# Pooled attention feeding a SoLU feed-forward block: SyncE's plain transfers moved to slots of their own, and one matmul group put first in every second slot

## The chip, the core and the metric

The kernel runs on one core of one Trainium2 chip. The metric is the device time of one launch in microseconds (us), the median of several runs. TensorE (PE) multiplies matrices, VectorE (DVE), ScalarE (ACT) and GpSimd (POOL) work element by element, SyncE (SP) only issues DMAs. All engines run their own instruction lists and wait for each other by semaphores.

## What is computed

```python
# q: (4, 12288, 128), kv: (4, 384, 32, 128), w_sr: (128, 128)
kv_pool = kv.reshape(B, H // 4, 4, W // 4, 4, C).mean(axis=(2, 4))
k = v = kv_pool.reshape(B, -1, C) @ w_sr               # 768 keys a batch
a = softmax(q @ k.T / sqrt(C))
x = (a @ v).reshape(B * S, 128)                        # 49152 tokens
h = x @ w_in                                           # 128 -> 1024
solu = h * softmax(h)
ln = (solu - mean(solu)) / sqrt(var(solu) + 1e-6) * g_ln
out = ln @ w_out                                       # 1024 -> 128
```

## The kernel before

The 49152 tokens are cut into 384 tiles of 128 tokens, 96 to each of the four batches, and four tiles make a group. One hand-written loop runs over 384 slots. The order in which the program text emits instructions is the order in which each engine gets them; no scheduler changes it. A slot holds one tile's worth of every stage, each stage working on another tile: the scores `s` of the tile after the slot's own (`scores_pe`), its softmax (`scores_exp`, `scores_split`, which write `phl`), the hidden layer `h` of the tile nine slots back (`hidden_pe`), its SoLU one to two slots later (`hidden_max`, `hidden_exp`, `hidden_u`, then POOL's `hidden_high` and `hidden_low`, which write `uhl`), and the output product `o` of the tile fourteen slots back (`final_pe`).

Values in fp16 are kept as a high and a low part, so each product is three matmuls: in a slot PE runs 6 matmuls for `s`, 6 for `h`, 24 for `o`, and a share of the 18 that form the attention output `xa` of a whole group (`values`). The first 5 of these 18 stand in a group's second slot, since `xa` needs the transposed probabilities `pT` of all four tiles of its group.

In this text a group's slots are called first, second, third and fourth (slot number modulo 4 is 0, 1, 2, 3). In PE's list a slot reads `s`, a piece of `xa`, `h`, `o`; in the second slot it was `s`, 5 `xa`, `h`, `o`. `h` may start when DVE has read the scores out of the PSUM buffer that it takes over (`phl`, L619).

SP's list carries two DMA transposes a slot, `pT` (L622) and `uT` (L777), in that order, and three kinds of plain transfers: the queries (`qf`, `q_load`, L528) once a group, the output (`out_dram<-ob`, `final_out`, L860) once a group, and at the start the first loads. The keys and values of the next batch (`kv_load`, L227, 384 KB each, 42 of them in the loop) are issued by ACT, from its own DMA queue. `kv_plan` says in which slot each is loaded and in which later slots POOL adds it up; `LATE` holds two exceptions. An SP instruction that waits holds up all that stand behind it.

`uT` is read by `o` three slots after the slot that issues it, `pT` of a group's fourth tile by `xa` two slots after.

Of the kernel before, what the change touches and what calls it, by code (L numbers as in the profile page):

```python
# [30 lines left out]
NT = B * TPB  # L31
GT = 4
# [29 lines left out]
FIT_AT = 302  # L62

SOON = {0: (), 1: (8, 8), 2: (8, 8), 3: (27, 33), 4: (39, 45), 5: (51, 54)}
LATE = {6: (12, 16, 18), 7: (16, 20, 22)}


@with_exitstack
def kernel(
# [429 lines left out]
    def kv_plan(b):  # L499


        for pos in range(RR):


            if b == 1 and pos in SOON:
                for half, slot in enumerate(SOON[pos]):
                    yield slot, [partial(kv_add, b, half, pos)]
                continue
            slot = 6 * pos - (28 if b == 1 else 30)
            load, *adds = (slot // GT * GT, slot + 3, slot + 5)  # L510
            if b == 1 and pos in LATE:
                load, *adds = LATE[pos]
            yield load, [partial(kv_load, b, pos)]
            if pos:
                for half, add in enumerate(adds):
                    yield add, [partial(kv_add, b, half, pos)]
        for slot, half, *fs in key_steps(b):
            yield slot, [partial(f, b, half) for f in fs]
# [4 lines left out]
    def q_load(g):  # L523
        if g >= NG or g % QL:
            return
        b, gb = divmod(g, GPB)
        t = dmt.tile([P, QL * 512], F32, tag="qf", name=f"qf_{g}", bufs=3)
        nc.sync.dma_start(t, qT[b, :, gb * 512 : (gb + QL) * 512])  # L528
        state["qf", g // QL] = t
# [315 lines left out]
        nc.gpsimd.tensor_tensor(f, f2, state.pop(("v3", g)), op=ALU.add)  # L845
        nc.gpsimd.tensor_tensor(f2, f, mhalf[:, :GT], op=ALU.pow)

    def final_out(g, to=None):
        _, f = state["f", g]
        ob = dmt.tile([P, GT, P], F32, tag="ob", name=f"ob_{g}")  # L850
        nc.vector.scalar_tensor_tensor(  # L851
            ob,
            state["po", g].rearrange("p (j c) -> p j c", j=GT),
            swi,
            f.unsqueeze(2).to_broadcast([P, GT, P]),
            op0=ALU.mult,
            op1=ALU.mult,
        )
        rows = out[g * GT * P : (g + 1) * GT * P, :] if to is None else to
        nc.sync.dma_start(rows.rearrange("(p j) c -> p (j c)", j=GT), ob.rearrange("p j c -> p (j c)"))  # L860

# [216 lines left out]
    for slot in range(NT):  # L1078
        i = slot - LH
        av, qtr = divmod(slot - LAV - GT + 1, GT)  # L1080
        tb, ti = divmod(slot, TPB)
        if ti == 12 and tb + 1 < B:
            kv_alloc(tb + 1)
        qs = GT if slot < 2 * GT else 2 * GT + 1 if slot < 3 * GT else 3 * GT + QSP
        todo = plan.pop(slot, [])
        at(slot, scores_exp)
        for f in held:
            f()
        held = []
        if slot <= LH:  # L1090
            at(slot - 1, scores_split)
        at(i - 1, hidden_u)
        at_last(slot - XSP - 1, values_split)
        if slot < 9:
            for f in fill.pop(slot, []):
                f()
        if 0 <= av < NG:
            values(av, qtr, 0)
        if slot != 8:
            at(slot + 2 if slot < 8 else slot + 1, scores_pe)  # L1100
        at_soon(slot - NORM, values_norm)
        at_last(slot - FSC, final_scale)
        at(i - 1, hidden_high)
        at(i - 1, hidden_low)
        at_last(slot - FSC, final_root)
        if slot < NT and 0 < qs < slot and (slot - 1 - qs) % GT == 0:
            q_low(slot // GT + 1)
        if slot < NT and 0 < qs <= slot + 1 and (slot + 1 - qs) % GT == 0:
            q_scale((slot + 1) // GT + 1)
        if slot < NT - 1:  # L1110
            at(i - 1, hidden_var)
        at(i, hidden_max)
        at(i, hidden_exp)
        if slot == NT - 1:
            hidden_var(i - 1)
        for f in fill.get(slot, []):
            f()
        pairs = [st for st in todo if len(st) > 1 and st[0].func is not kv_add]
        for st in pairs:
            st[0]()  # L1120
        if 0 <= av < NG:
            values(av, qtr, 1)
        for st in pairs:
            held += st[1:]
        if slot >= LH:
            at(slot, scores_split)
        at_soon(slot - NORM, values_recip)
        at_soon(slot - NORM, values_recip_u)
        at(i + 1, hidden_pe)
        if slot < NT - 1:  # L1130
            at(slot - LO, final_pe)
        at(i - 1, hidden_turn)
        if slot % GT == GT - 1:
            q_load(slot // GT + 3)
        at_last(slot - LO - 1, final_out)
        at_last(slot - XSP, values_out)
        for st in todo:
            if st[0].func is kv_add:
                for f in st:
                    f()  # L1140
            elif len(st) == 1:
                st[0]()
        if slot < NT and 0 < qs <= slot and (slot - qs) % GT == 0:
            q_split(slot // GT + 1)
# [183 lines left out]
```

## Time and profile before

| | |
|---|---|
| time, median of 3 runs | 1843.82 us (1843.07 to 1850.48) |
| profiled execution: its time | 1843.65 us |
| its span, first to last instruction | 1841.9 us |
| PE busy | 1818.3 us (99%) |
| DVE, ACT, POOL busy | 1761.9, 1742.6, 1667.2 us |
| granted TensorE clock, mean | 0.998 |
| DMA | 432.80 MB, 235 GB/s |

The profile comes from one execution. Busy time counts an engine's own instructions, not its waits, and a busy PE need not be at its peak, since matmuls overlap. The chain of waits goes back from the last instruction, at each step to what released it or to its engine's instruction before, and so shows which engine sets the pace in a stretch.

### The profile page before, as it was taken

To read this page: it belongs to the slowest core of one execution; us is meant where nothing else is said; L and a number is where in the kernel's file an instruction comes from. 1 tells how busy PE (TensorE), PEld (TensorE's weight loads), DVE (VectorE), ACT (ScalarE), POOL (GpSimd) and SP (SyncE) were. 2 spreads that over 40 slices of the span, in tenths; PEclk is the share of its full clock that TensorE was granted. 3 is DMA by queue.
4 is the path that set the end of the run, shared out by engine and by line. 5 is a ranking of instruction groups with operands and counts; after the bars stand their busy time and mean duration, and the time that the engine had idled before them with its cause. 6 is when DMAs were issued, how large, how long until landed. Compare 5 with 4: busy or idle time off the path is not lost.

```text
span 1841.9 us, 42770 instructions
## 1 busy us (share of the span) xinstructions
PE 1818.3 (99%) x15747; PEld 1218.5 (66%) x15747; DVE 1761.9 (96%) x2635; ACT 1742.6 (95%) x3129; POOL 1667.2 (91%) x1466
## 2 busy tenths in 40 slices
PE   8999999999999999999999999999999999999998
PEld 5577777777666666666666666666666666666666
DVE  6999999999999999999999998999999999999997
ACT  5999999999999999999999998999999999999997
POOL 5899999899999999989999998998988988888887
PEclk9999999999999999999999999999999999999999
DMA  9999999999999999999999999999999999999997
GB/s 301 203 249 230 230 253 232 247 230 237 242 241 241 246 245 242 246 235 235 247 239 241 242 222 230 247 239 224 222 233 230 232 235 231 220 235 224 230 223 168
DMA packets 1440027, 432.80 MB, mean 235 GB/s; under 512 B 1404608, under 2 KB 1408832, under 8 KB 1439552
## 3 DMA queue, kind: packets, MB, share of 16 engines
q1 hardware_dynamic: 1433616, 413.45, 112.6%
q10 hardware_dynamic: 6192, 16.52, 3.2%
q8 instruction: 126, 2.06, 0.5%
q14 instruction: 93, 0.76, 0.1%
HBM read 52.50 MB, written 25.17 MB: 42 GB/s over the span
## 4 chain that ended last, share of the span: by engine, by line
PE 46%; DVE 26%; ACT 15%; issue 9%; DMA 2%; POOL 1%; SPq 0%; DVEq 0%; ACTq 0%; POOLq 0%
PE o L828 13%; PE h L700 13%; PE s L587 10%; PE xa L647 10%; DVE junkd L708 8%; DVE phl L619 6%; DVE nm L608 5%; ACT e L724 4%; ACT junk L803 4%; DVE u L738 3%; ACT phl L611 3%; ACT s L609 2%; DVE ob L851 2%; DVE xl L659 2%; DMA kv<-in_kv_dram 1%
## 5 line engine op out<-in xcount | busy, mean ns | idle before, releaser
L762 POOL TENSOR_TENSOR uhl<-u,uhl 128x1024 f16<-128x1024 f32 x382 | 815.0, 2134 | 32.3 <-ACT uhl L753 0.6
L828 PEld LDWEIGHTS <-uT 128*128 128x128 f16 x9072 | 537.9, 98 | 89.1 <-issue 0.9
L828 PE MATMUL o<-wch,uT 128*128 128x128 f16 x6048 | 568.1, 219 | 0.1
L828 PE MATMUL o<-wcl,uT 128*128 128x128 f16 x3024 | 526.1, 219 | 0.0
L738 DVE SCALAR_TENSOR_TENSOR u<-h,rz,e 128x1024 f32<-128x1024 f32 x384 | 490.4, 1277 | 33.3 <-ACT e L724 32.7
L708 DVE TENSOR_SCALAR_CACHE_REDUCE junkd<-h,rz 128x1024 bf16<-128x1024 f32 x384 | 490.7, 1278 | 7.6 <-PE h L700 7.2
L647 PE MATMUL xa<-pT,vhl 128*128 128x512 f16 x1728 | 470.4, 380 | 5.4 <-DMA pT<-phl 5.4
L755 POOL TENSOR_SCALAR uhl<-u 128x1024 f16<-128x1024 f32 x379 | 395.8, 1044 | 83.9 <-DVE u L738 72.7
L724 ACT ACTIVATE e<-h,nm,rz 128x1024 f32<-128x1024 f32 x384 | 458.5, 1194 | 8.2 <-DVE junkd L708 8.2
L803 ACT ACTIVATE junk<-u,su 128x1024 bf16<-128x1024 f32 x384 | 438.0, 1141 | 0.1
L609 ACT ACTIVATE s<-s,nm 128x768 f32<-128x768 f32 x384 | 334.7, 872 | 47.6 <-DVE nm L608 47.1
L619 DVE SCALAR_TENSOR_TENSOR phl<-s,phl 128x768 f16<-128x768 f32 x384 | 365.8, 953 | 6.5 <-ACT phl L611 4.1
L608 DVE TENSOR_REDUCE nm<-s 128x1 f32<-128x768 f32 x384 | 360.1, 938 | 9.1 <-PE s L587 4.6
L611 ACT ACTIVATE phl<-s 128x768 f16<-128x768 f32 x384 | 311.1, 810 | 12.1
L700 PEld LDWEIGHTS <-xh 128*128 128x128 f16 x1536 | 144.0, 97 | 195.4 <-issue 27.1
L647 PEld LDWEIGHTS <-vhl 128*128 128x128 f16 x1728 | 162.4, 98 | 141.3 <-issue 16.0
L700 PE MATMUL h<-w_in_h,xh 128*128 128x512 f16 x768 | 228.9, 380 | 3.6 <-DVE rz L682 3.2
L700 PE MATMUL h<-w_in_l,xh 128*128 128x512 f16 x768 | 229.0, 380 | 0.0
L700 PE MATMUL h<-w_in_h,xl 128*128 128x512 f16 x768 | 228.8, 380 | 0.0
L587 PEld LDWEIGHTS <-qh 128*128 128x128 f16 x1152 | 122.6, 114 | 42.9
L587 PE MATMUL s<-kh,ql 128*128 128x384 f16 x576 | 140.8, 326 | 0.1
L587 PE MATMUL s<-kl,qh 128*128 128x384 f16 x576 | 140.8, 326 | 0.0
(153 smaller groups left out, 1820.4 us busy)
## 6 DMA issues: line engine op xcount, KB each, us to landing
qf<-in_q_dram SPq DMA_DIRECT2D x96, 256.0 KB, 3.8
out_dram<-ob SPq DMA_DIRECT2D x96, 256.0 KB, 2.9
kv<-in_kv_dram ACTq DMA_DIRECT2D x42, 384.0 KB, 4.3
kv<-in_kv_dram SPq DMA_DIRECT2D x22, 384.0 KB, 7.5
pT<-phl SPq DMA_TRANSPOSE x384, 4.0
uT<-uhl SPq DMA_TRANSPOSE x378, 4.6
raw_in<-in_moe_w_in_dram SPq DMA_DIRECT2D x1, 1024.0 KB, 5.1
raw_out<-in_moe_w_out_dram SPq DMA_DIRECT2D x1, 1024.0 KB, 9.6
```

The lines of the kernel that those rows point to most:

```text
L587: nc.tensor.matmul(s[:, half, :384], tokens(lh)[:, j, :], rh[:, half * 384 : (half + 1) * 384], start=n == 0, stop=n == 2,)
L608: nc.vector.tensor_reduce(nm, s, axis=AX.XY, op=ALU.max, negate=True)
L619: nc.vector.scalar_tensor_tensor(phl[:, 1], state.pop(("s", t)), SC, phl[:, 0], op0=ALU.mult, op1=ALU.subtract)
L647: nc.tensor.matmul(xa, v[:, c, :], pT[:, :, a * NKC + c, :], start=n == 0, stop=n == len(seq) - 1)
L700: nc.tensor.matmul(h[:, hs], lh[:, ts], rh[:, hs], start=n == 0, stop=n == 2)
L708: nc.vector.tensor_scalar(junk, state["h", t], state["rz", g][1][:, j : j + 1], None, op0=ALU.mult, op1=ALU.min, accum_out=nm,)
L724: nc.scalar.activation(e, state["h", t], AF.Exp, bias=nm, scale=state["rz", g][0][:, js], accum_out=state["z2", g][:, js],)
L738: nc.vector.scalar_tensor_tensor(u, state.pop(("h", t)), state["rz", g][2][:, j : j + 1], state.pop(("e", t)), op0=ALU.mult, op1=ALU.mult, ...
L755: nc.gpsimd.tensor_scalar(uhl[:, 0, :], u, 1.0, 1.0, op0=ALU.mult, op1=ALU.mult)
L762: low.tensor_tensor(uhl[:, 1, :], u, uhl[:, 0, :], op=ALU.subtract)
L803: nc.scalar.activation(junk, u, AF.Square, scale=-float(DFF), bias=su, accum_out=state["v3", g][:, j : j + 1],)
L828: nc.tensor.matmul(po[:, ts], uT[:, a * NFC + c, :], w[:, c, :], start=start, stop=stop)
```

## The change

Four things move. The query load of a group goes from behind the fourth slot's transposes to behind the next (first) slot's. The output store is taken out of `final_out` into `final_store`, which runs one slot later: behind the fourth slot's transposes and no longer behind the third's. The key loads go from ACT's list in the first slot to SP's list in the second, behind its transposes. On PE, in a group's second slot, the order becomes `s`, `o`, `h`, `xa`. What each instruction computes, and how many there are, stays.

```diff
-LATE = {6: (12, 16, 18), 7: (16, 20, 22)}
+LATE = {6: (13, 16, 18), 7: (17, 20, 22)}
...
-            load, *adds = (slot // GT * GT, slot + 3, slot + 5)
+            load, *adds = (slot // GT * GT + 1, slot + 3, slot + 5)
...
-            yield load, [partial(kv_load, b, pos)]
+            yield load, [partial(kv_load, b, pos, nc.sync)]
...
-    def final_out(g, to=None):
+    def final_out(g, to=None, later=False):
...
+        state["ob", g] = ob
+        if not later:
+            final_store(g, to)
+
+    def final_store(g, to=None):
+        ob = state.pop(("ob", g))
         rows = out[g * GT * P : (g + 1) * GT * P, :] if to is None else to
         nc.sync.dma_start(rows.rearrange("(p j) c -> p (j c)", j=GT), ob.rearrange("p j c -> p (j c)"))
...
-        if 0 <= av < NG:
+        o_first = slot % GT == 1
+        if o_first:
+            at(slot - LO, final_pe)
+        elif 0 <= av < NG:
             values(av, qtr, 1)
...
         at(i + 1, hidden_pe)
-        if slot < NT - 1:
+        if o_first:
+            if 0 <= av < NG:
+                values(av, qtr, 1)
+        elif slot < NT - 1:
             at(slot - LO, final_pe)
         at(i - 1, hidden_turn)
-        if slot % GT == GT - 1:
-            q_load(slot // GT + 3)
-        at_last(slot - LO - 1, final_out)
+        at_last(slot - LO - 2, final_store)
+        if slot and slot % GT == 0:
+            q_load(slot // GT + 2)
+        at_last(slot - LO - 1, partial(final_out, later=True))
```

SP's list before, from the third slot of one group to the third of the next (slots 230 to 234, in the third batch):

```order
L622 DMA_TRANSPOSE pT_16382<-phl_16504 128x12x128
L777 DMA_TRANSPOSE uT_16566<-uhl_16516 128x16x128
L860 DMA out_dram<-ob_16568 128x512
L622 DMA_TRANSPOSE pT_16382<-phl_16574 128x12x128
L777 DMA_TRANSPOSE uT_16638<-uhl_16590 128x16x128
L528 DMA qf_16640<-in_q_dram 128x512
L622 DMA_TRANSPOSE pT_16673<-phl_16646 128x12x128
L777 DMA_TRANSPOSE uT_16707<-uhl_16659 128x16x128
L622 DMA_TRANSPOSE pT_16673<-phl_16717 128x12x128
L777 DMA_TRANSPOSE uT_16787<-uhl_16734 128x16x128
```

The same slots after the change (L866 is the store, L227 a key load that ACT issued before):

```order
L622 DMA_TRANSPOSE pT_16380<-phl_16504 128x12x128
L777 DMA_TRANSPOSE uT_16566<-uhl_16516 128x16x128
L622 DMA_TRANSPOSE pT_16380<-phl_16573 128x12x128
L777 DMA_TRANSPOSE uT_16637<-uhl_16589 128x16x128
L866 DMA out_dram<-ob_16568 128x512
L622 DMA_TRANSPOSE pT_16671<-phl_16644 128x12x128
L777 DMA_TRANSPOSE uT_16705<-uhl_16657 128x16x128
L528 DMA qf_16707<-in_q_dram 128x512
L622 DMA_TRANSPOSE pT_16671<-phl_16715 128x12x128
L777 DMA_TRANSPOSE uT_16785<-uhl_16732 128x16x128
L227 DMA kv_12_16788<-in_kv_dram 128x768
```

The store stood ahead of the fourth slot's `pT` and now stands behind that slot's `uT`; the queries and keys each come a slot apart from it.

PE's list in a second slot (slot 233) before, the first row or two of each product; what a row waits for stands in brackets:

```order
L587 MATMUL s_16723<-kh_7595,ql_16499 128x384
L647 LDWEIGHTS vhl_7597 [waits DMAHW5_49,DMAHW2_49,DMAHW0_49]
L647 MATMUL xa_16744<-pT_16382,vhl_7597 128x512 [waits DVE_49]
L700 LDWEIGHTS xh_16709 [waits DVE_49,Activation_49]
L700 MATMUL h_16756<-w_in_h,xh_16709 128x512 [waits PE_49]
L828 LDWEIGHTS uT_16566 [waits DMAHW3_49]
L828 MATMUL o_16541<-wch,uT_16566 128x128
```

And after the change:

```order
L587 MATMUL s_16721<-kh_7593,ql_16499 128x384
L828 LDWEIGHTS uT_16566 [waits DMAHW3_49]
L828 MATMUL o_16541<-wch,uT_16566 128x128
L700 LDWEIGHTS xh_16709 [waits DVE_49,Activation_49]
L700 MATMUL h_16772<-w_in_h,xh_16709 128x512 [waits PE_49]
L647 LDWEIGHTS vhl_7595 [waits DMAHW7_49,DMAHW4_49]
L647 MATMUL xa_16779<-pT_16380,vhl_7595 128x512 [waits DMAHW2_49]
```

The wait for `uT` (a DMA) now comes right behind `s`, the wait for `pT` (DMAs too) last in the slot.

## Rows read from the trace of the kernel before

**Rows 1.** The page's part 1: busy time, share of span, instructions.
```profile
PE 1818.3 (99%) x15747; PEld 1218.5 (66%) x15747; DVE 1761.9 (96%) x2635; ACT 1742.6 (95%) x3129; POOL 1667.2 (91%) x1466
```
**Rows 2.** Waits: who waited for whom; us in total, times, longest us.
```profile
PE xa L647 <- DMA pT<-phl: 5.4, 2, 2.7
```
**Rows 3.** Timeline, ACT, an instruction that comes once a group: start us, duration us.
```profile
1067.26 0.38 ACT L838 ACTIVATE f<-z,bb 128x4 f32<-128x4 f32 x1
...
1085.65 0.38 ACT L838 ACTIVATE f<-z,bb 128x4 f32<-128x4 f32 x1
...
1125.07 0.38 ACT L838 ACTIVATE f<-z,bb 128x4 f32<-128x4 f32 x1
...
1166.28 0.38 ACT L838 ACTIVATE f<-z,bb 128x4 f32<-128x4 f32 x1
...
1499.97 0.38 ACT L838 ACTIVATE f<-z,bb 128x4 f32<-128x4 f32 x1
...
1518.36 0.38 ACT L838 ACTIVATE f<-z,bb 128x4 f32<-128x4 f32 x1
```
**Rows 4.** Chain of waits around 1098 us: start us, us, what.
```profile
1091.24 7.05 DMA pT<-phl
...
1099.67 1.29 PE h L700 x6
1100.96 1.34 PE o L828 x24
1102.30 0.98 PE s L587 x6
1103.28 1.08 PE xa L647 x5
```
**Rows 5.** Timeline around two waits of PE; SPq and ACTq rows are DMA issues.
```profile
1073.76 0.33 ACTq L227 DMA_DIRECT2D kv<-in_kv_dram  x1
...
1088.63 1.90 SPq L777 DMA_TRANSPOSE uT<-uhl  x1
...
1090.62 0.53 SPq L860 DMA_DIRECT2D out_dram<-ob  x1
...
1092.14 0.33 ACTq L227 DMA_DIRECT2D kv<-in_kv_dram  x1
...
1098.43 1.24 PE L647 MATMUL xa<-pT,vhl 128*128 128x512 f16 x5 [2.72 <-DMA pT<-phl]
...
1137.94 1.91 PE L647 MATMUL xa<-pT,vhl 128*128 128x512 f16 x5 [2.70 <-DMA pT<-phl]
```
**Rows 6.** Windows: stretch, us, busy by engine, granted clock, DMA share, GB/s.
```profile
1138.40:1141.80 3.40, 3.40 (x10) 1.16 (x9) 0.00 (x0) 1.58 (x3) 3.32 (x3) 0.50 1.21 246
```
**Rows 7.** Timeline from 1509 us, a second slot in the last batch, and what follows.
```profile
1509.87 1.24 PE L647 MATMUL xa<-pT,vhl 128*128 128x512 f16 x5
1509.91 0.95 DVE L619 SCALAR_TENSOR_TENSOR phl<-s,phl 128x768 f16<-128x768 f32 x1
...
1511.01 0.59 PE L700 MATMUL h<-w_in_h,xh 128*128 128x512 f16 x2
...
1511.87 0.60 PE L700 MATMUL h<-w_in_h,xl 128*128 128x512 f16 x2
...
1512.92 1.28 DVE L708 TENSOR_SCALAR_CACHE_REDUCE junkd<-h,rz 128x1024 bf16<-128x1024 f32 x1
```
**Rows 8.** Chain of waits from 1500 to 1540 us: shares by line.
```profile
by line: issue 18.8%; DVE junkd L708 18.1%; DVE phl L619 13.1%; DVE nm L608 10.8%; ACT junk L803 8.5%; ACT e L724 8.4%; DVE u L738 7.7%; ACT phl L611 6.1%; DVE xl L659 3.3%; DVE ob L851 3.3%; ACT f L838 2.1%; ACT s L609 1.1%; DVE rz L682 0.
```
**Rows 9.** Groups of instructions: PE's first matmuls of h; busy, mean ns, idle before.
```profile
L700 PE MATMUL h<-w_in_h,xh 128*128 128x512 f16 x768 | 228.9, 380 | 3.6 <-DVE rz L682 3.2 <-DVE phl L619 0.3
```
**Rows 10.** SP's own waits: us in total, times, longest us.
```profile
SPq L777 <- POOL uhl L755: 341.0, 238, 5.5
```
**Rows 11.** The tile uT, all 378 transposes of it.
```profile
DMA to landing us min/median/max: 3.6/4.6/9.1
```
**Rows 12.** The tile pT, all 384 transposes of it.
```profile
DMA to landing us min/median/max: 3.2/4.0/7.3
```

## The prediction

> **What bounds the kernel now.** I read the busy times first, then the period of a group, then the chain of waits, then the waits of PE. PE is busy 99% of the span [rows 1], which alone says only that it is hardly ever empty. Whether it is at its floor is told by the length of a group. In a stretch of the chain that runs on PE alone, `s` takes 0.98 us, `o` 1.34, `h` 1.29, and 5 matmuls of `xa` 1.08 [rows 4]. Four slots and 18 matmuls of `xa` are then 4 x 3.61 + 18/5 x 1.08 = 14.44 + 3.89 = 18.33 us. The groups really take 18.39 us: an instruction that ACT runs once a group stands at 1499.97 and at 1518.36 [rows 3]. So in an undisturbed group PE is 0.06 us above its floor, and what sets the 18.39 is not PE: from 1500 to 1540 us the chain holds DVE and ACT and no PE at all [rows 8]. Two loops, PE's and that of DVE and ACT, have nearly the same length. Little is to be had from either while the other stays.
>
> What is left are disturbed groups. The two from 1085.65 to 1125.07 took 39.42 us, 2.64 more than 2 x 18.39; the two from there to 1166.28 took 41.21, 4.43 more [rows 3]. In each pair PE waited once, 2.72 and 2.70 us, at the first matmul of `xa`, for a transpose `pT` to land [rows 5]; these two are all such waits of PE in the run, 5.4 us together [rows 2]. Behind the second the granted clock was 0.50 for 3.40 us [rows 6], the lower of the two levels, 1.2 GHz: half of 3.40, 1.70 us, is lost once more, and 2.70 + 1.70 is the 4.4 that the second pair is long. **Both together cost 2.64 + 4.43 = 7.07 us.** That is what I count on; the rest of the kernel has no idle time of this size.
>
> **Why these transposes were late.** The first was issued at 1091.24 and landed 7.05 us later [rows 4], where the median is 4.0 and the longest 7.3 [rows 12]. Two plain transfers were about: SP issued the store at 1090.62, right ahead of it, and ACT issued a key load of 384 KB at 1092.14, while the transpose was in flight [rows 5].
>
> **The change part by part.** *Store.* It no longer stands ahead of the fourth slot's `pT`, which can then be issued 1091.24 - 1090.62 = 0.62 us sooner [rows 5]. *PE's order.* In the second slot `o` and `h` now run ahead of `xa`, which asks for `pT` 1.34 + 1.29 = 2.63 us later [rows 4]. *Keys.* They go out two slots before the next `pT` that matters, so its flight may shrink from 7.05 towards the median of 4.0: 0 to 3.05 us [rows 4, 12]. The waits were 2.72 and 2.70. Store and order together relieve 3.25, so both waits go, with 0.53 us to spare, even if the flight stays at 7.05; with the keys gone the spare is up to 3.6. No wait, no fall of the clock behind it: -7.07 us.
>
> The Trainium skill speaks against the move of the keys ("DMA: Bandwidth & Descriptors", section "Issuing engines are not separate DMA queues"): transfers issued by Scalar, Sync or GpSimd run on the same 16 engines and interleave, and another issuer saves sequencer time alone. By that rule the keys on SP gain nothing by their queue, and the flight would stay at 7.05; by the rows it shortens because the moment is another. The sum is 1836.6 either way, but by the rule it hangs on the 0.53 us.
>
> *`h` in the second slot.* It waits for `phl`, which ends at 1509.91 + 0.95 = 1510.86, and starts at 1511.01; PE was through with `xa` at 1509.87 + 1.08 = 1510.95 and so lost 0.06 us [rows 7]. With `o` in that place PE arrives at 1509.87 + 1.34 = 1511.21: `h` starts 0.20 later and finds `phl` done. The last matmul of `h` then ends at 1511.87 + 0.60 + 0.20 = 1512.67, and DVE, which reads it from 1512.92 [rows 7], still has 0.25 us. Nothing becomes late. PE leaves the slot 0.06 sooner; what this is worth lies between 0 and 96 x 0.06 = 5.8 us. PE's idle time ahead of `h`, 3.6 us in all [rows 9], lies inside that bound. I take 0, because the chain of an undisturbed group does not touch PE [rows 8]: it will wait the 0.06 elsewhere.
>
> *ACT without the key issues.* 42 issues of 0.33 us are 13.9 us of its queue. The group from 1067.26 to 1085.65 had such an issue, at 1073.76 [rows 5], and took 18.39 us [rows 3], as long as the group without one. So 0 of them were on the path: 0 gained.
>
> *SP with the key issues.* About 0.55 us (a plain issue took 0.53 [rows 5]) in 42 of 96 groups. SP waits 341.0 us for one of POOL's two steps alone [rows 10], 3.4 us in a group of 18.4, which covers it. Behind the key load stand the third slot's `pT` and `uT`. That `pT` is one of four that `xa` needs, but the fourth is issued a slot (4.6 us) after it and decides. The third slot's `uT` is what `o` reads at its new place: issued at 1088.63, in one of the most delayed groups, it would be wanted behind `s`, at 1098.43 - 2.72 = 1095.71, 7.1 us later [rows 5]; it takes 4.6 in the median, 9.1 at most [rows 11]. With 0.55 for the key issue: 5.2 against 7.1, no wait; at the longest flight 9.65 - 7.1 = 2.6 us. I take 0, since the median fits and other groups have more room, and keep 2.6 for the rivals.
>
> *Queries, POOL and the start.* Queries come a slot later and are first read four slots on; key loads are read by POOL two slots after issue at the least, 9.2 us, more than the longest `pT`: 0. In slot 13 no `o` exists yet, so 4 matmuls of `xa` that covered a wait of `h` go behind it: 4/5 x 1.08 = 0.9 us at most, once; I take 0, DVE being late there.
>
> **Sum.** The profiled execution took 1843.65 us, of which 1841.9 is its span; what lies around it (1.75) stays. 1843.65 - 7.07 = 1836.58. The median of the runs is 1843.82, 0.17 above the profiled one, so the forecast is **1836.6 us**, 0.39% below the median.
>
> **Rivals.** (1) *More:* PE is the pace in more of the run than the stretch of rows 8, and gets back its 0.06 us in every second slot and part of its waits for `h`: 1836.6 - 5.8 = 1830.8. For it: PE ran the chain alone right behind the first wait [rows 4]. Against: rows 8.
> (2) *Nothing:* it was not the neighbours that made `pT` late but SP, which stood behind POOL [rows 10]; with one more issue on its list it comes later still, or the keys now delay something else as much. Then two waits of this size stay: 1843.6. Against: 3.25 us of relief do not depend on the flight.
> (3) *Slower:* the keys sit on SP's queue ahead of the third slot's `uT`, and `o`, now first behind `s`, waits for it. It decides where that flight exceeds 7.1 - 0.55 = 6.5 us; the median is 4.6, the longest 9.1 [rows 11]. At the price of 2.6 us in a third of the 42 groups with keys, 14 x 2.6 = 36: 1873. The skill has a rule for it (same page, section "Queues, rings and completion order"): on one ring descriptors are taken in order, so nothing behind the keys can pass them. That price would be the full 2.6 only if the transfer of the keys took that long; no row here shows keys on SP among the slots.
>
> **How the numbers follow.** Forecast 62%; more 20%; nothing 11%; slower 7%. A measurement of this kernel can tell some 0.5% (9.2 us) from no change, which puts the bounds at 1834.6 and 1853. Faster: rival 1 and the lower edge of the forecast, 0.23. Slower: rival 3, 0.07. Within: 0.70, the likeliest case among them. The range goes from 1831, the full 5.8 of the unknown gain, to 1844, the case in which nothing is gained; rival 3 and a little beyond rival 1 are left out.
>
> **What would show it.** Right: no wait of PE at `xa` for `pT`; no stretch at a clock of 0.50 in the middle of the run; groups of 18.39 us throughout the third batch; `h` in a second slot some 0.2 us behind `phl`, without idle time. A period under 18.36 in the last batch would mean rival 1. PE idle at `o` in second slots, released by a DMA of `uT`, would mean rival 3; at `xa`, or ACT waiting to write `phl`, rival 2. The forecast is wrong if any of these waits comes to more than 2 us in all.

## The result, and the profile after

The changed kernel took 1860.03 us (median of 6 runs, 1854.24 to 1865.99), the kernel before beside it 1845.53 (6 runs, 1841.04 to 1850.48): a ratio of 1.0078, with a 95% interval of 1.0049 to 1.0107. So it is slower, by 14.5 us, where the prediction had 1836.6 and a range of 1831 to 1844. The profiled execution took 1865.99 us, 1864.2 of it span. It is the slowest of the six, 22.3 us behind the profiled execution of the kernel before, so what the two traces show beside each other is more than the 14.5 us.

The page of the changed kernel, its parts 1, 4 and 5 (the last: busy us, mean ns, then idle time before and what ended most of it):

```profile
PE 1823.3 (98%) x15747; PEld 1218.7 (65%) x15747; DVE 1768.2 (95%) x2635; ACT 1745.6 (94%) x3129; POOL 1667.6 (89%) x1466
...
DVE 28%; POOL 24%; PE 18%; issue 13%; ACT 12%; DMA 5%; SPq 0%; POOLq 0%; DVEq 0%; ACTq 0%
...
L828 PE MATMUL o<-wch,uT 128*128 128x128 f16 x6048 | 569.1, 219 | 13.2 <-DMA uT<-uhl 13.0
...
L647 PE MATMUL xa<-pT,vhl 128*128 128x512 f16 x1728 | 465.9, 379 | 0.5 <-DMA pT<-phl 0.5
```

The work is nearly the same (compare [rows 1]), the idle time is not. The two waits that the prediction went after are gone: 5.4 us at `xa` [rows 2] are now 0.5. In their place stand others. The waits of the changed kernel, us in total, times, longest, from the answers for PE, POOL, DVE and ACT:

```profile
PE o L828 <- DMA uT<-uhl: 13.0, 12, 2.0
...
PE s L587 <- DVE u L738: 5.8, 10, 0.9
PE s L587 <- POOL ql L574: 5.1, 8, 0.6
...
POOL ka L238 <- DMA kv<-in_kv_dram: 32.6, 14, 4.5
...
DVE rz L682 <- POOL zz L674: 16.4, 12, 2.4
...
ACT phl L611 <- DMA pT<-phl: 9.6, 10, 2.4
```

Two of them are new in kind. PE waits 12 times at `o` for a transposed `u`: the prediction's third rival. And POOL waits 14 times for keys, up to 4.5 us, where before it had no such wait among the slots; that stood in no rival. What POOL then delivers late, DVE and PE wait for (`rz` by 16.4 us, where before it waited 0.2).

Where the loss lies is told by the once-a-group instruction of [rows 3], in the changed kernel's timeline of ACT (start us, duration us):

```profile
590.92 0.38 ACT L838 ACTIVATE f<-z,bb 128x4 f32<-128x4 f32 x1
611.40 0.38 ACT L838 ACTIVATE f<-z,bb 128x4 f32<-128x4 f32 x1
629.90 0.38 ACT L838 ACTIVATE f<-z,bb 128x4 f32<-128x4 f32 x1
648.99 0.38 ACT L838 ACTIVATE f<-z,bb 128x4 f32<-128x4 f32 x1
...
1411.49 0.38 ACT L838 ACTIVATE f<-z,bb 128x4 f32<-128x4 f32 x1
1429.88 0.38 ACT L838 ACTIVATE f<-z,bb 128x4 f32<-128x4 f32 x1
```

In the last batch, which loads no keys, a group takes 18.39 us as before. Among the loads of keys (some 290 to 1320 us) groups take 20.48, 18.50 and 19.09. Nearly all of the loss is there: the changed kernel is 0.15 us behind at 303 us and 21.8 at 1243. Keys are loaded ahead of 303 us too, from 76 us on, and cost nothing there. A group takes 18.73 us in that stretch in both kernels, and from 130 to 290 us the chain of the kernel before holds PE alone.

One such place, in the changed kernel's timelines of SP, POOL and PE (start us, us; in brackets idle time before and its releaser):

```profile
1106.90 0.57 SPq L528 DMA_DIRECT2D qf<-in_q_dram  x1
1107.56 1.70 SPq L622 DMA_TRANSPOSE pT<-phl  x1
1109.35 2.48 SPq L777 DMA_TRANSPOSE uT<-uhl  x1
1111.88 0.58 SPq L227 DMA_DIRECT2D kv<-in_kv_dram  x1
1112.55 2.72 SPq L622 DMA_TRANSPOSE pT<-phl  x1
1115.37 3.45 SPq L777 DMA_TRANSPOSE uT<-uhl  x1
1118.92 1.42 SPq L622 DMA_TRANSPOSE pT<-phl  x1
...
1109.92 2.13 POOL L762 TENSOR_TENSOR uhl<-u,uhl 128x1024 f16<-128x1024 f32 x1
...
1117.82 1.00 POOL L238 TENSOR_TENSOR ka<-ka,kv 128x384 f32<-128x384 f32 x1 [4.51 <-DMA kv<-in_kv_dram]
...
1120.97 0.23 PE L828 MATMUL o<-wch,uT 128*128 128x128 f16 x1 [1.75 <-DMA uT<-uhl]
```

The keys go out at 1111.88, and POOL stands still for 4.51 us until 1117.82: it was ready for them at 1113.31, 1.4 us after their issue, where the prediction had 9.2. POOL is ahead of SP. The transpose of the `uhl` that POOL ended at 1109.92 + 2.13 = 1112.05 is issued only at 1115.37, and PE waits for it until 1120.97. And SP does not rest here: 1111.88 + 0.58 is 0.09 before 1112.55, 1112.55 + 2.72 is 0.10 before 1115.37, and so on. It doesn't wait for its data; it works through a list that is late.

The kernel before is much the same in this. Its timeline of SP, and one row of ACT's, over part of a group:

```profile
1014.94 1.46 SPq L622 DMA_TRANSPOSE pT<-phl  x1
1016.50 1.70 SPq L777 DMA_TRANSPOSE uT<-uhl  x1
1018.25 0.58 SPq L528 DMA_DIRECT2D qf<-in_q_dram  x1
1018.94 1.42 SPq L622 DMA_TRANSPOSE pT<-phl  x1
1020.45 4.35 SPq L777 DMA_TRANSPOSE uT<-uhl  x1
1024.89 1.43 SPq L622 DMA_TRANSPOSE pT<-phl  x1
...
1018.60 0.34 ACTq L227 DMA_DIRECT2D kv<-in_kv_dram  x1
```

In stretches of 100 us between 300 and 1200 us, SP's issues take 92.0 to 94.9% of the time in this kernel (89.2 to 92.2% from 1400 to 1700 us, without keys), and the gaps between them are 0.09 us in the median. That is the state in which the change put 42 issues more on SP's list. Note also the two rows at 1018.25 and 1018.60: queries (SP) and keys (ACT) go out within 0.35 us of each other. The diff doesn't say that they do; the experiments show that it matters.

The kernel before has its exceptions, too. The two loads of keys that went out furthest from queries are the two ahead of its two waits, at 1092.14 [rows 5] and at 1131.67. Queries followed 5.7 us later, and a store stood 1.5 us ahead of each (at 1090.62 [rows 5] and at 1130.22); no other load of keys between 290 and 1320 us is within 3 us of a store.

```profile
1097.85 0.57 SPq L528 DMA_DIRECT2D qf<-in_q_dram  x1
...
1130.22 0.53 SPq L860 DMA_DIRECT2D out_dram<-ob  x1
...
1131.67 0.34 ACTq L227 DMA_DIRECT2D kv<-in_kv_dram  x1
...
1137.34 0.57 SPq L528 DMA_DIRECT2D qf<-in_q_dram  x1
```

Whether the distance made SP late or a late SP made the distance, these rows can't tell.

### The profile page after: what moved, and what is told of

Read it like the earlier page. It is cut to its first block, busy times and chain, and to the rows that moved or that the text cites. A ratio compares the mean times of both kernels' runs of the same rounds, so it can differ in the third digit from the quotient of the medians.

```text
span 1864.2 us, 42727 instructions
## 1 busy us (share of the span) xinstructions
PE 1823.3 (98%) x15747; PEld 1218.7 (65%) x15747; DVE 1768.2 (95%) x2635; ACT 1745.6 (94%) x3129; POOL 1667.6 (89%) x1466
## 4 chain that ended last, share of the span: by engine, by line
DVE 28%; POOL 24%; PE 18%; issue 13%; ACT 12%; DMA 5%; SPq 0%; POOLq 0%; DVEq 0%; ACTq 0%
POOL uhl L762 10%; DVE junkd L708 8%; DVE phl L619 6%; POOL uhl L755 6%; PE o L828 5%; DVE nm L608 5%; PE h L700 5%; DVE u L738 4%; PE s L587 4%; PE xa L647 4%; ACT e L724 3%; ACT junk L803 3%; DMA uT<-uhl 3%; ACT phl L611 3%; POOL ka L238 2%
## 5 line engine op out<-in xcount | busy, mean ns | idle before, releaser
L587 PE MATMUL s<-kh,qh 128*128 128x384 f16 x576 | 140.9, 326 | 4.6 <-DVE u L738 4.5
```

The lines of the kernel that those rows point to most:

```text
L587: nc.tensor.matmul(s[:, half, :384], tokens(lh)[:, j, :], rh[:, half * 384 : (half + 1) * 384], start=n == 0, stop=n == 2,)
```

## The experiments

Each kernel ran beside the kernel before on the same chip; the medians of before were 1846.2, 1844.3, 1843.9, 1845.6 and 1845.0 in the five series, in the order of the groups below. One run of before lies anywhere from 1836.8 to 1860. The ratios are not the quotients of the medians: for `plain_alone` the medians differ by 0.20% and the ratio is 1.0047, for `o_alone` it is the other way round.

**First: the change in its parts.** The three theories at that time were: A, SP's list is full; B, the keys come too late for POOL; C, `o` comes too early in the second slot.

The changed kernel with the keys back on ACT:

```diff
...
-            load, *adds = (slot // GT * GT + 1, slot + 3, slot + 5)
+            load, *adds = (slot // GT * GT, slot + 3, slot + 5)
...
-            yield load, [partial(kv_load, b, pos, nc.sync)]
+            yield load, [partial(kv_load, b, pos)]
```

> The changed kernel with the key loads back on ACT, in a group's first slot; store, queries and o ahead of h and xa stay moved. Theory A (SP's list is full: it issues 94% of the time already before the change, and every key load put on it makes all transposes behind it late): no wait of POOL for keys, PE's wait at o for uT under 2 us, 1836 to 1840 us. Theory B (keys are fetched too late for POOL, the queue does not matter): the same 1836 to 1840, POOL's wait for keys gone. Theory C (o stands too early in the second slot): PE still waits 10 us or more at o for uT, 1850 to 1858.

Measured: 1859.8 us, ratio 1.0058 (1.0026 to 1.0089). Against A and B as the only causes: the keys are where they were, and the loss stays. PE waits 13.0 us at `o` for `uT`, as C has it.

The kernel before with only the keys moved (the edit above, the other way round):

> The kernel before with one part of the change: key loads on SP, in a group's second slot. Theory A: SP runs 3 us further behind its data, 1853 to 1862, with waits at xa for pT, at the phl buffers, and of POOL for keys. Theory B: POOL waits some 30 us for keys, 1853 to 1862. Theory C: no harm, 1840 to 1846.

Measured: 1856.8 us, 1.0052 (1.0033 to 1.0072). The keys alone lose 10.6 us, though POOL waits for them for no more than 2.4 us in all.

The kernel before with only store and queries moved (the diff of the change without its lines on keys and `o`):

> The kernel before with the output store and the query loads of a group moved a slot later on SP, the keys on ACT, PE's order as before. Theories A, B and C alike: the number of issues on SP is unchanged, the store no longer stands ahead of the fourth pT: 1838 to 1845, waits at xa shorter by 0.6 us each.

Measured: 1849.9 us, 1.0047 (1.0019 to 1.0074).

The kernel before with only `o` ahead of `h` and `xa` in the second slot:

> The kernel before with one part of the change: in a second slot o ahead of h and xa on PE. Theories A and B: the waits at xa for pT shrink by up to 2.6 us each and o finds its uT landed: 1837 to 1846. Theory C: PE waits at o for uT, over 10 us in all, 1850 to 1858.

Measured: 1854.8 us, with runs from 1835.6 to 1866.2, 1.0020 (0.9980 to 1.0059): no verdict. In the profiled run PE and ACT wait for `pT`, and for `uT` only 1.4 us in all, against C:

```profile
PE xa L647 <- DMA pT<-phl: 15.6, 8, 3.4
...
ACT phl L611 <- DMA pT<-phl: 15.1, 10, 3.2
```

So each part lost something or nothing, none gained, and the parts together lost more than the whole: 10.6 + 3.8 + 8.6 = 23.0 us by the medians, against 14.5, though the last two are known to within 5 to 7 us at best. That speaks for a cause which any one part sets off.

**Second: is it time in SP's list?** A theory D joined: bytes, that is the bandwidth of the DMA engines.

The kernel before with 42 transfers of 64 bytes that nobody reads, on SP in the second slots:

```diff
...
             yield load, [partial(kv_load, b, pos)]
+            yield load // GT * GT + 1, [partial(kv_tiny, b, pos)]
```

> The kernel before, with 42 transfers of 64 bytes more on SyncE, each in the second slot of the group whose key load stands in its first (the keys stay on ScalarE, and nothing reads the 64 bytes). Three theories for the 10.6 us that keys_alone lost against before (1856.8 against 1846.2): A, SyncE's list is full in the stretches with keys (93.7 to 94.6% of the time in issues, about 93 ns between them), so 42 issues of some 0.6 us that are put there, 25 us in all, push its transposes back until TensorE waits; B, the keys come too late for GpSimd's adds; D, the DMA engines are the limit there, and what counts is bytes. A expects the loss of keys_alone again: 1851 to 1860, transposed u issued 2 to 4.5 us behind its data there where before has 1.5 to 2. B and D expect before's time: 1843 to 1849.

Measured: 1856.9 us, 1.0062 (1.0038 to 1.0087). To add 64 bytes cost as much as to move 384 KB of keys, which the kernel before loads elsewhere, to the same place: D falls. But keys and queries fell apart here as well (12 of 33 together, see the table), so the 12.6 us need not all be the 64 bytes' own. The trace shows what they do. DMA of that kernel in 8 us from 990, GB/s in 40 equal slices of 0.2 us:

```profile
GB/s 253 287 282 282 274 243 205 216 255 279 280 274 274 287 284 278 260 94 63 269 292 291 289 291 276 178 183 269 276 282 292 285 284 284 275 329 392 369 246 226
```

And its timeline of SP there:

```profile
990.21 1.73 SPq L782 DMA_TRANSPOSE uT<-uhl  x1
991.99 0.43 SPq L234 DMA_DIRECT2D tiny<-in_kv_dram  x1
992.51 1.27 SPq L627 DMA_TRANSPOSE pT<-phl  x1
```

The transposes run at 280 to 292 GB/s. The 64 bytes are issued at 991.99, and in the slices from 993.4 the stream of transposes breaks off, 94 and 63 GB/s, before it runs on. So even 64 bytes among the transposes cost a pause.

The kernel before with the queries of two groups in one transfer (`QL = 2`, two buffers of twice the size):

> The kernel before, with the queries of two groups in one transfer of twice the size: 48 issues fewer on SyncE, some 27 of them in the stretches with keys (0.6 us each, 17 us there), the same bytes. A (SyncE's list full) expects a gain: transposed u issued under 1 us behind its data in the stretches with keys, as in the last batch (0.8), and 1836 to 1842. D (bytes) and B (keys late) expect before's time: 1843 to 1849.

Measured: 1861.1 us, 1.0094 (1.0060 to 1.0128). A miss for A: 48 issues fewer, and slower. Some 6.5 us of it were lost in the first seven groups, where the larger load stands in the way of the start, so this run is not a clean test; but the rest of it was no gain either.

The changed kernel with the same:

> The changed kernel (1860 against 1845.5), with the queries of two groups in one transfer. A expects that 27 issues fewer against the 42 that the keys added give back more than half of the loss: 1846 to 1853. B: the keys are no earlier but for what SyncE's list gains; 1855 to 1860. D: 1857 to 1862. The order of o in the second slot (theory C, o too early there) would keep 5 us or more of the loss: 1850 or above with waits of TensorE at o for the transposed u left.

Measured: 1867.0 us, 1.0133 (1.0095 to 1.0170). A miss for A again.

The changed kernel with the keys (all but two loads) one group earlier:

```diff
-            load, *adds = (slot // GT * GT + 1, slot + 3, slot + 5)
+            load, *adds = (slot // GT * GT + 1 - GT, slot + 3, slot + 5)
```

> The changed kernel, with every key load still on SyncE and in a second slot, but of the group before: GpSimd's add has 18.4 us more for it. B (keys too late: GpSimd waited 14 times for 32.6 us in the changed kernel) expects these waits gone and 1846 to 1851. A (the list is full, whenever the keys stand in it) and C expect GpSimd's waits gone too, but TensorE still late at o and xa: 1855 to 1860.

Measured: 1851.7 us, 1.0033 (1.0012 to 1.0054). POOL's waits for keys are gone, and with them 7 to 8 of the 14.5 us; PE's waits at `o` are not (21.4 us, 17 times, in a profiled run of 1862.3, the slowest of its twelve). B is a part, not the whole.

**Third: alone or together.** From the traces came theory E: a plain load that comes to the DMA engines alone costs them a pause, and loads in flight together share it. In the profiled run of before, 26 of 33 key loads (290 to 1320 us) are issued between 1.0 us before and 1.6 us after a load of queries; after the change, none of 33.

The kernel before, keys on SP directly behind the queries:

```diff
...
-            load, *adds = (slot // GT * GT, slot + 3, slot + 5)
+            load, *adds = (slot // GT * GT - 1, slot + 3, slot + 5)
...
-            yield load, [partial(kv_load, b, pos)]
+            yield load, [partial(kv_load, b, pos, nc.sync)]
```

> The kernel before, with the keys on SyncE in the fourth slot, directly behind the queries' load. The traces of the runs so far give a theory E: the DMA engines are what is short, and each plain transfer that comes to them by itself makes them pause: about the 64-byte transfers of sp_tiny the packets in flight fall from about 20 to 1 or 2 for 0.4 to 0.5 us, about a lone query load for about 1 us, while keys and queries that are in flight together share one pause. In before the keys (ScalarE, first slot) land beside the queries (SyncE, fourth slot just ahead), after the change they do not. E expects this kernel no slower than before, 1838 to 1847, though SyncE has 42 issues more. A (SyncE's list is full, whatever is beside what) expects the loss of keys_alone and sp_tiny: 1853 to 1860.

Measured: 1847.9 us, 1.0020 (1.0004 to 1.0037). Nearly as E has it, a little over its upper bound. The same 42 issues on SP as in keys_alone, and a loss of 4.0 us where that had 10.6.

The kernel before, keys on ACT but in the second slot of the group before (`slot // GT * GT + 1 - GT`):

> The kernel before, with the keys still on ScalarE, but in the second slot of the group before, so that they land two slots away from the queries, and early enough for GpSimd. SyncE's list is that of before. E (pauses of their own) expects most of the loss of keys_alone and sp_tiny: 1851 to 1859, transposed u issued 3 us and more behind its data in the stretches with keys. A expects before's time: 1841 to 1848.

Measured: 1857.0 us, 1.0071 (1.0047 to 1.0094). SP's list is untouched, the keys are early, and the loss is that of keys_alone. A and B can't explain this run.

The kernel before with the 64 bytes directly behind the queries:

> The kernel before, with the 42 transfers of 64 bytes of sp_tiny (1856.9), but each in the fourth slot directly behind the queries' load and not in the second. As many issues on SyncE as sp_tiny. E expects before's time to within 3 us: 1842 to 1848. A expects sp_tiny's: 1853 to 1860.

Measured: 1838.5 us, 0.9979 (0.9958 to 1.0000). The same transfers as sp_tiny, in another place: 18 us less. This settles it between A and E, against A. That it is even below before, E doesn't explain.

The changed kernel with the keys directly behind the queries, in the first slot:

> The changed kernel (1860), with the keys, still on SyncE, in the group's first slot directly behind the queries, and not in the second; store, queries and the order of o as changed. E expects most of the loss back: 1845 to 1852, with no more than what the order of o and the moved store and queries cost by themselves (plain_alone 1849.9, o_alone 1854.8 with a wide interval). A expects no change: 1857 to 1862.

Measured: 1847.8 us, 1.0017 (0.9996 to 1.0038): a loss of 3.9 us where the changed kernel had 14.5, by one slot's move of the keys. (The keys are a slot earlier as well, so what keys_early gained is part of it.)

What the pause is can be read from three windows of 8 us, again GB/s in slices of 0.2. In keys_alone, a lone load of queries, issued at 941.01 (window from 941), and a lone load of keys, issued at 985.54 (window from 985):

```profile
GB/s 288 289 291 291 289 292 333 120 164 297 358 241 147 183 230 150 239 291 288 292 204 195 275 269 285 255 268 279 239 248 260 260 291 196 285 284 276 266 202 260
...
GB/s 263 282 285 289 284 282 280 285 287 360 265 123 61 123 138 230 335 339 320 293 189 113 157 291 292 292 282 280 289 160 283 288 296 288 291 291 341 477 338 333
```

In key_at_q, both, issued at 988.48 and 989.11 (window from 988):

```profile
GB/s 268 293 282 278 282 291 287 289 275 209 41 164 297 338 297 174 287 333 420 370 325 279 279 106 78 264 291 291 292 306 268 236 58 8 9 8 168 293 289 294
```

A dip stands ahead of the data of each load and another one or two behind it. Queries and keys apart make two such pairs, together one (the near-zero slices at the end are a fetch of instructions).

How much this is can be worked out from the transposes' packets in the 5 us behind each issue from 300 to 1300 us, against their full rate of 289 GB/s, without the windows that hold a fetch of instructions (medians of 9 to 21 windows). In a second slot without a plain transfer 0.4 to 0.5 us of transposing are lost (keys_alone, before), with 64 bytes 0.7 (sp_tiny), with keys 2.2 (keys_alone). Behind queries alone 1.4 are lost, behind queries and keys 2.9 (key_at_q). So keys cost the transposes 1.7 to 1.8 us alone and 1.5 beside queries, and 64 bytes alone 0.2. What a meeting saves is then some 0.2 to 0.3 us a load, 8 to 13 us for 42 loads if all of it is on the path. That is of the size of the 10.6 us of keys_alone, and 42 times the 0.2 of the 64 bytes is 8 of the 12.6 of sp_tiny; that these times are on the path is argued, not shown.

A rival remains: not the company but the place in the group. What was put among the transposes by itself (keys_alone, key_apart_act, sp_tiny) stood in the second slot, and what was put together in the fourth or first; no kernel here has queries and keys together in the second. Against this rival stand plain_alone, which left the keys in their slot and took the queries away, and lost, and o_tiny_at_q below.

**Fourth: the store, and the order of `o`.**

The kernel before with store, queries and keys in a row on SP:

> The kernel before, with store, queries and keys directly behind one another on SyncE, all in the fourth slot (store moved one slot back, queries where they were, keys from ScalarE to SyncE); o as before. E (each plain transfer that comes to the DMA engines by itself costs a pause; those together share one) expects one pause fewer in each group than key_at_q (1847.9): 1835 to 1843, below before. The rival: the three, 896 KB, are too long a block ahead of the next transposes, and TensorE waits for them at xa: 1848 to 1858.

Measured: 1869.1 us, 1.0114 (1.0082 to 1.0147): the slowest of all, and a miss for E in its plain form. PE waits at `xa`:

```profile
PE xa L647 <- DMA pT<-phl: 18.0, 21, 2.0
```

The kernel before with the store directly ahead of the queries (store's lines of the change, queries left):

> The kernel before, with only the store moved, one slot back, so that it stands on SyncE directly ahead of the queries in the fourth slot; keys on ScalarE and o as before. E expects 1835 to 1844, if the keys go on landing beside the queries. If the store's place is of no matter: before's time, 1841 to 1848.

Measured: 1855.2 us, 1.0042 (1.0014 to 1.0070). Not better with the store beside the loads, but worse; keys and queries drifted apart in part (18 of 33 together).

key_at_q with the order of `o` of the change:

> key_at_q (1847.9) with o ahead of h and xa in the second slot, as in the change. If the order of o itself costs time (theory C, TensorE waits at o for the transposed u, at its new place): 1853 to 1860. If o_alone lost only because keys and queries drifted apart: 1843 to 1849, with runs closer together than those of o_alone (1835.6 to 1866.2).

Measured: 1844.6 us, 0.9988 (0.9968 to 1.0008), runs from 1839.7 to 1849.3. Here the order of `o` costs nothing, and PE waits at `o` for 0.9 us in all.

The changed kernel with store, queries and keys in a row in the first slot (one of its 96 stores is left out):

> The changed kernel, with the keys directly behind the queries in the first slot (as after_key_at_q, 1847.8), and the store one slot later still, directly ahead of the queries; o ahead of h and xa as changed. E expects one pause fewer in each group than after_key_at_q: 1836 to 1845. If the store's place is of no matter, or the block is too long: 1846 to 1856.

Measured: 1860.0 us, 1.0073 (1.0044 to 1.0103). A miss for E again: ACT waits 24.9 us for `pT`, and PE 8.7 at `o` for `uT`.

**Fifth: two last points.** tiny_at_q with the order of `o`:

> tiny_at_q (1838.5: 64 bytes behind each queries' load in the fourth slot, keys on ScalarE as in before) with o ahead of h and xa in the second slot. If the order of o costs nothing as long as keys and queries go together (as o_key_at_q has it): 1834 to 1842, below before. If it costs by itself, or makes SyncE late enough that keys and queries drift apart again as in o_alone: 1847 to 1860.

Measured: 1854.6 us, 1.0040 (1.0006 to 1.0074). The second of the two expectations: in its profiled run only 2 of 33 key loads are issued beside the queries (tiny_at_q: 26). ACT issues the keys, SP the queries, and as SP falls behind, the two drift apart. The same in o_alone, where 3 of 33 are together, here 6.1 us apart:

```profile
1034.51 0.34 ACTq L227 DMA_DIRECT2D kv<-in_kv_dram  x1
...
1040.59 0.57 SPq L528 DMA_DIRECT2D qf<-in_q_dram  x1
```

The kernel before with the 64 bytes directly behind the store:

> The kernel before, with the 42 transfers of 64 bytes of sp_tiny directly behind the store in the third slot. Where the group has one (keys in the next group's first slot by the plan's grid), a read follows the write at once. If any two plain transfers that are together share one pause: 1840 to 1848, as tiny_at_q. If a read shares only with a read, and pays its own pause behind a write: 1851 to 1860, as sp_tiny (1856.9).

Measured: 1851.2 us, 1.0025 (0.9997 to 1.0054), between the two expectations and with runs from 1836.9 to 1860.7: inconclusive.

Side by side, by how many of the 33 (32 where the loads are a group earlier) key loads between 290 and 1320 us of the profiled run are issued beside queries, as above, and beside a store (by the same bounds). The counts are of one execution, whose time stands beside them:

| kernel | beside queries | beside a store | that run, us | median us | ratio to before |
|---|---|---|---|---|---|
| before | 26 | 2 | 1843.7 | 1843.9 to 1846.2 | |
| after | 0 | 0 | 1866.0 | 1860.0 | 1.0078 |
| keys_back | 0 | 7 | 1861.5 | 1859.8 | 1.0058 |
| keys_alone | 0 | 0 | 1857.0 | 1856.8 | 1.0052 |
| plain_alone | 0 | 22 | 1846.7 | 1849.9 | 1.0047 |
| keys_early | 0 | 0 | 1862.3 | 1851.7 | 1.0033 |
| q_pairs_after | 0 | 0 | 1862.3 | 1867.0 | 1.0133 |
| o_tiny_at_q | 2 | 26 | 1858.3 | 1854.6 | 1.0040 |
| o_alone | 3 | 19 | 1858.1 | 1854.8 | 1.0020 |
| key_apart_act | 7 | 0 | 1853.3 | 1857.0 | 1.0071 |
| q_pairs | 11 | 2 | 1857.5 | 1861.1 | 1.0094 |
| sp_tiny | 12 | 6 | 1860.8 | 1856.9 | 1.0062 |
| store_at_q | 18 | 22 | 1848.7 | 1855.2 | 1.0042 |
| tiny_at_store | 22 | 3 | 1855.4 | 1851.2 | 1.0025 |
| tiny_at_q | 26 | 0 | 1842.3 | 1838.5 | 0.9979 |
| after_key_at_q | 33 | 0 | 1850.6 | 1847.8 | 1.0017 |
| key_at_q | 33 | 0 | 1846.5 | 1847.9 | 1.0020 |
| o_key_at_q | 33 | 0 | 1842.8 | 1844.6 | 0.9988 |
| one_place | 33 | 33 | 1870.8 | 1869.1 | 1.0114 |
| after_one_place | 33 | 33 | 1860.5 | 1860.0 | 1.0073 |

Where keys and queries go together in all loads, or in as many as in before, and no store is near, the kernel is between 5.4 us below before and 4.0 above it. Where they are apart it loses, by little in plain_alone's median and without a verdict in o_alone. Where a store goes with both in every load (one_place, after_one_place) it loses 23 and 14 us.

## Why the prediction was wrong

The step that failed is the price of the moved keys, which the prediction put at 0 in three places: in SP's time, in POOL's 9.2 us, and in what they do to the transposes. The two waits that it was after did go.

**The two waits: right, and of no use.** Both waits at `xa` went, as the terms for store and order had it (5.4 us became 0.5), and the fall of the clock with them. The row of [rows 3] at 1125.07 opens the group in which the kernel before has its second wait; the row that ends that group, and the same two of the changed kernel:

```profile
1147.66 0.38 ACT L838 ACTIVATE f<-z,bb 128x4 f32<-128x4 f32 x1
...
1149.55 0.38 ACT L838 ACTIVATE f<-z,bb 128x4 f32<-128x4 f32 x1
...
1167.94 0.38 ACT L838 ACTIVATE f<-z,bb 128x4 f32<-128x4 f32 x1
```

The changed kernel is 1149.55 - 1125.07 = 24.5 us behind ahead of that group and 1167.94 - 1147.66 = 20.3 behind after it, in 18.39 us: those 4.2 us, nearly the 4.43 of the prediction, were gained. In the group of the first wait the changed kernel lost 1.1 us more than the other, by waits of its own. But key_at_q, tiny_at_q and plain_alone, which keep the order of `o`, are 1.7 to 2.4 us shorter than before in the group of the first wait and 4.2 in that of the second, too, two of them with the store in its old place. So the waits went, but that store and order removed them is not shown.

**"SP waits 341.0 us ... which covers it": misread.** The row of [rows 10] was taken for idle time of SP. It isn't: the row takes POOL's last signal before an issue is through, and sums the time from the end of SP's instruction before to that signal, time in which SP was already issuing. The trace shows it: each of the 378 issues of a `uT` starts after POOL had ended its `uhl`, by 0.03 us at the least. In stretches of 100 us between 300 and 1200 us, a `uT` was issued 0.9 to 3.4 us (medians) behind its data before, and 2.3 to 5.6 after. The 42 issues of some 0.6 us thus had little cover. They are not the price by themselves, though: key_at_q has them too and lost 4 us, and tiny_at_q has 42 issues more and lost nothing. What the misreading hid is that SP was late, on which the next two points rest.

**"The keys gain nothing by their queue" was right; their moment was priced on one side only.** The prediction asked what the keys did to one `pT` beside them, and never what lay beside the keys. In before they went out with the queries; moved, they came to the transposes by themselves. key_apart_act moved them on ACT's queue and lost 13.1 us; key_at_q moved them to SP's, together with the queries, and lost 4.0. This is what the Trainium skill says ("DMA: Bandwidth & Descriptors", section "Issuing engines are not separate DMA queues": the queues of the issuing engines share the same 16 engines): the runs agree, the issuer mattered less than the moment, 4.0 us against 13.1. The other rule (same page of the Trainium skill, section "Queues, rings and completion order": on one ring descriptors are started in their order) was named for rival 3; the changed kernel's trace agrees, since of the three DMAs that SP issued behind each of the 42 key loads none landed before it, but the 64 bytes of sp_tiny show that the length of the transfer ahead was not what counted. That the meeting matters by a pause that is shared rests on the 0.2 to 0.3 us a load worked out above: it is argued, and the kernels with a store in the row speak against its plain form.

**"9.2 us, more than the longest `pT`: 0": wrong.** Two slots by the list of a kernel are two slots of one engine, and the engines do not stand in the same slot at one time. In the kernel before POOL's first add of the keys of 1073.76 [rows 5] comes 15.9 us after ACT's issue, for three slots by the list:

```profile
1089.66 1.00 POOL L238 TENSOR_TENSOR ka<-ka,kv 128x384 f32<-128x384 f32 x1
```

In the changed kernel two slots lie between, 4.6 us less, but the keys now stand at the end of a slot's list on SP, which is late: in the 14 cases POOL was ready for them 1.4 to 3.1 us after their issue, they took 3.8 to 6.0 to land, and it waited 32.6 us. keys_early puts 7 to 8 us of the loss on it.

**Rival 3** named PE's wait at `o`, and it came, 12 times and 2.0 us at most, near the 2.6 in its price and the 14 in its count. But its chance was 7%, its sum (36 us) took all of them at the longest flight, where the 12 came to 13.0 us, and its cause was one `uT` behind one key load, where in fact SP's whole list is late. With the loads beside each other, o_key_at_q, the order of `o` costs nothing. It costs in o_tiny_at_q, where ACT issues the keys and SP the queries (o_alone, with the same split, gave no verdict). That the drift comes about because PE, no longer waiting for `pT` so soon, lets SP fall further behind, is argued, not shown.

**Rival 1** was wrong: the last batch has 18.39 us a group in both kernels, and the stretch up to 303 us 18.73 in both, so nothing came of the 0.06 us. **The range** was too narrow on its upper side because what SP's late list could cost was set to 0 by a misread row, and because the two terms that could be worse, 2.6 us a group, were kept out of it as a rival.

Left open: why 64 bytes behind the queries (tiny_at_q) made the kernel 0.2% faster, with an interval that touches 1; why a store beside the loads loses what a load beside a load gains, whether because it writes or because the three together are a long block ahead of the next `pT`; and why plain_alone, with no keys beside queries and 22 of 33 beside a store, lost only 3.8 us by its median (by its ratio, 1.0047, some 9). No kernel that was tried is a sure gain over before.

## What to carry to other kernels

When one engine issues nearly all transfers, look at its timeline for rest before pricing an issue at nothing: a row that says whom it waited for last is no proof that it was idle. Ask of a transfer that is to be moved what it is in flight with, not only what it is in the way of; here, whether two loads left within about a microsecond of each other, by two engines and by no one's plan, counted for more than the queue that they stood in. Where such a meeting matters, put both on one queue in a row, since two engines' lists drift apart. And when a reader is said to come two slots after a load, read that distance from the trace of both engines, not from the program.

## What had not been expected of the hardware

A 64-byte transfer among a stream of DMA transposes took the stream from about 285 GB/s to 94 and 63 GB/s for two slices of 0.2 us. Adding 42 of them cost 12.6 us of run time (1856.9 against 1844.3), more than to move 42 loads of 384 KB to the same slots (10.6, keys_alone), while beside the queries they cost nothing (1838.5 against 1843.9); in the first of these kernels keys and queries fell apart as well, so the 12.6 us are not all theirs for certain. A fetch of instructions by the DMA engines (16 KB, every 14 us or so) brings the transposes nearly to a stand for over a microsecond: in the median of the 68 between 300 and 1300 us of the kernel before, they fall from some 285 to 12 GB/s or less for 1.3 us. In the kernel before, 3 us from 1026 (slices of 0.075 us):

```profile
GB/s 283 297 294 270 482 270 263 266 273 266 143 20 3 0 0 0 0 0 7 7 7 10 10 7 14 7 10 10 61 276 280 290 290 294 290 290 294 290 290 287
...
q8 instruction: 1, 0.02, 2.1%
```

From the slice at 1026.8 to that at 1028.1 next to nothing moves, and SP's issue of a `uT` at 1026.42 takes 3.24 us, where the one at 1016.50 above took 1.70.
